# Moving SyncE's second load ahead of its opening-barrier instruction in a decode kernel

## The chip, the cores and the metric

The kernel runs on one core of a Trainium2 chip. The metric is the device time of one execution in microseconds (us). Most executions of one kernel agree within about 0.3%, but some fall into a slower state that is about 8 us longer. A run is called slow when it is over 1.5% above the fastest of the same kernel.

## The reference, cut to what matters

One decode step of a conditioned transformer block, for a batch of 8: a modulation from `c`, attention of one new token over a cache of 8192 positions (32 query heads, 4 key/value heads), and a gated MLP, all bf16.

```python
mod = (silu(c) @ w_mod).reshape(8, 6, 1, -1)          # w_mod: 1024 x 6144, 12 MB
sa, ca, ga, sb, cb, gb = (mod[:, i] for i in range(6))
h = layernorm(x) * (1 + ca) + sa
x = x + ga * attention(h, k_cache, v_cache, wq, wo)   # caches: 2 x 64 MB
h = layernorm(x) * (1 + cb) + sb
x = x + gb * mlp(h, W_gate, W_up, W_down)             # 3 x 7 MB
```

Every weight and cache byte is read once: 185.6 MB. (In the comments of the code an MB is 2^20 bytes; in the text MB and GB are decimal.) That is nearly all of the work.

## The kernel before

All large loads go through SyncE, in one fixed order, into one buffer in SBUF (the on-chip memory) called `arena`. The first three load `w_mod`. The first of them is small.

```python
load(("wm", 0),  wm_src[:, 0:D], D, 0)              # load 1: 128 rows of 2 KB,  256 KB
load(("wm0", 0), wm_src[:, D:24 * D], 23 * D, D)    # load 2: 128 rows of 46 KB, 5888 KB
load(("wm", 1),  wm_src[:, 24 * D:48 * D], 24 * D, 24 * D)   # load 3: rows of 48 KB, 6144 KB
# then wq in two halves; the second half overwrites part of w_mod's first half, so it
# waits until the first w_mod matmuls are done; then K and V of each batch, wo, gate, up, down
```

ScalarE issues two loads of 16 KB for `c` and `x`, 32 rows of 512 B each. The matmuls on `w_mod` need a vector that is computed from `c`; on the tensor engine they also stand behind the layernorm of `x`.

A program opens with a barrier. Each engine gives a signal (its drain instruction), GpSimd collects the signals and releases all, and each engine waits for the release (an EventSemaphore). A helper moves the first loads, which need no wait, ahead of this barrier:

```python
def start_loads_first(nc, n):
    ...
    for engine, ahead, total in ((SP, 1, n), (Activation, 2, 2)):   # names shortened
        ...
        first = [...][:total]                       # the first `total` loads of this engine
        ...
        at = where(rest, engine, "EventSemaphore")[0]
        rest = rest[:at] + first[ahead:] + rest[at:]            # ahead of the barrier's wait
        at = where(rest, engine)[0]
        block.instructions = rest[:at] + first[:ahead] + rest[at:]   # ahead of the drain too
...
start_loads_first(nc, 3)
```

So before the change SyncE runs: load 1, drain, load 2, load 3, wait.

Of the kernel before, what the change touches and what calls it, by code (L numbers as in the profile page):

```python
# [236 lines left out]
def start_loads_first(nc, n):  # L237

    block = nc.main_func.blocks[0]

    def where(ins, engine, opcode=None):
        return [i for i, x in enumerate(ins) if x.engine == engine and opcode in (None, x.opcode)]

    for engine, ahead, total in ((mybir.EngineType.SP, 1, n), (mybir.EngineType.Activation, 2, 2)):
        ins = list(block.instructions)
        at = where(ins, engine, "EventSemaphore")[0]
        first = [ins[i] for i in where(ins, engine) if i > at][:total]
        assert all(x.opcode == "DMACopy" and not x.sync_info.on_wait for x in first), [x.opcode for x in first]
        names = {x.name for x in first}
        rest = [x for x in ins if x.name not in names]  # L250
        at = where(rest, engine, "EventSemaphore")[0]
        rest = rest[:at] + first[ahead:] + rest[at:]
        at = where(rest, engine)[0]
        block.instructions = rest[:at] + first[:ahead] + rest[at:]
# [9 lines left out]
def bass_adaLN_cond__gqa_block_cached__glu_gated_reglu__decode_kernel(nc, A_x, A_k_cache, A_v_cache, A_wq, A_wo, B_x, B_W_gate, B_W_up, B_W_down, c, w_mod, out):  # L264
# [28 lines left out]
    with ExitStack() as es:  # L293
# [483 lines left out]
        P.plan()  # L777
        P.emit(nc, dict(sp=nc.sync, act=nc.scalar, pool=nc.gpsimd, dve=nc.vector, pe=nc.tensor), sems)
        start_loads_first(nc, 3)
        hold_weights(nc, holding)  # L780

# [27 lines left out]
```

## Time and profile before

| what | value |
|---|---|
| time, median of the first 3 runs | 436.74 us (436.25 to 444.89; the last is a slow run) |
| span of the profiled run | 435.1 us |
| bytes moved by DMA, mean rate | 185.74 MB, 427 GB/s |
| slices of 40 in which the DMA engines are at least 90% busy | 38 |

The page of the kernel before. The digits of the DMA row are the busy share of each fortieth of the span in tenths, and the row below is the rate in GB/s.

```profile
span 435.1 us, 4774 instructions
...
DMA  9999999999999999999999999999999999899995
GB/s 374 425 458 434 429 434 434 477 387 473 401 428 434 476 398 428 434 476 392 434 440 470 392 434 440 431 431 476 398 428 434 476 398 470 386 429 481 393 416 232
...
q1 hardware_dynamic: 5360, 185.61, 98.9%
```

SyncE's queue (q1) alone fills the 16 DMA engines for 98.9% of the span. The first slice moves 374 GB/s, less than its neighbours: that is the start-up, and the change is aimed at it.

The timeline of the kernel before, in pieces: start in us, duration in us, engine, source line, operation and count. SPq and ACTq are instructions that SyncE and ScalarE issue.

```profile
0.00 0.39 SPq L391 DMA_DIRECT2D arena<-in_w_mod_dram  x1
0.12 0.40 ACTq L423 DMA_DIRECT2D cx<-in_c_dram  x1
0.56 0.44 ACTq L423 DMA_DIRECT2D cx<-in_A_x_dram  x1
0.64 0.33 SPq L391 DMA_DIRECT2D arena<-in_w_mod_dram  x1
1.02 0.42 SPq L391 DMA_DIRECT2D arena<-in_w_mod_dram  x1
...
1.42 0.20 POOL L433 MEMSET identf<- 128x128 f32 x1 [0.98 <-POOLq L794]
...
8.58 0.58 PE L447 MATMUL ps<-cx,rsel 32*128 32x512 bf16 x1 [8.58 <-DMA cx<-in_A_x_dram]
...
23.38 0.33 SPq L391 DMA_DIRECT2D arena<-in_A_wq_dram  x1
```

Load 2 issues at 0.64. The first work after the barrier (GpSimd's memset) starts at 1.42. The first matmul waits for `x` until 8.58. The second half of `wq` can be issued only at 23.38, after the first `w_mod` matmuls.

The drains of the opening barrier in the same kernel (count, duration in ns, start in us to a tenth):

```profile
L794 SPq DRAIN  x1: 126/126/126, 0.4 to 0.4; - x1
L794 ACTq DRAIN  x1: 150/150/150, 1.0 to 1.0; - x1
```

The loads of the opening: size in KB, and us from issue to landing.

```profile
arena<-in_w_mod_dram SPq DMA_DIRECT2D x1, 5888.0 KB, 16.5
...
arena<-in_w_mod_dram SPq DMA_DIRECT2D x1, 256.0 KB, 2.7
...
cx<-in_A_x_dram ACTq DMA_DIRECT2D x1, 16.0 KB, 7.9
```

The 16 KB load of `x` takes 7.9 us to land because its packets take turns with 46 KB rows: on each engine its two rows and its closing packet of 4 B start at 4.1 to 4.6, 5.9 to 6.3 and 7.6 to 8.1 us, one after each row of load 2.

The trace also holds a record of each DMA packet (start, duration, size, queue). One row is one packet here. A 47,104-byte row at full speed takes 1.74 us on its engine. The records do not name the engine. Each load ends on each engine with a 4-byte packet, so the 16 ends of load 1 and the 16 first rows of load 2 can be sorted and set side by side:

```
kernel before, ns from the first issue, sorted:
load 1, its 4-byte packet ends:  1892 1953 2007 2053 2078 2092 2136 2146 2196 2207 2220 2267 2273 2334 2385 2391
load 2, its first row starts:    1942 2003 2057 2103 2127 2142 2186 2196 2246 2257 2270 2317 2323 2434 2469 2487
```

In 13 of the 16 pairs the row starts 49 or 50 ns after the packet that ends load 1, and in the other three 84 to 100 ns after it. (Sorted pairs need not be of one engine.) The 50 ns are not idle. The records show the load of `c` in them: two packets of 512 B and one of 4 B on each engine.

### The profile page before, as it was taken

To read this page: it belongs to the slowest core of one execution; us is meant where nothing else is said; L and a number is where in the kernel's file an instruction comes from. 1 tells how busy PE (TensorE), PEld (TensorE's weight loads), DVE (VectorE), ACT (ScalarE), POOL (GpSimd) and SP (SyncE) were. 2 spreads that over 40 slices of the span, in tenths; PEclk is the share of its full clock that TensorE was granted. 3 is DMA by queue.
4 is the path that set the end of the run, shared out by engine and by line. 5 is a ranking of instruction groups with operands and counts; after the bars stand their busy time and mean duration, and the time that the engine had idled before them with its cause. 6 is when DMAs were issued, how large, how long until landed. Compare 5 with 4: busy or idle time off the path is not lost. (4 is left out here: it accounts for less than half of the span.)

```text
span 435.1 us, 4774 instructions
## 1 busy us (share of the span) xinstructions
PE 259.8 (60%) x2139; PEld 136.1 (31%) x1979; DVE 249.3 (57%) x342; ACT 29.5 (7%) x54; POOL 8.8 (2%) x22
## 2 busy tenths in 40 slices
PE   0425239667837875883887478487837857263056
PEld 0100003164217224521822352183236217140015
DVE  1503049757972985697299549739963974421020
ACT  2000010100020001002000200200020020100000
POOL 3000000000000000000000000000000000000000
PEclk9976658969978995998799699869979997775669
DMA  9999999999999999999999999999999999899995
GB/s 374 425 458 434 429 434 434 477 387 473 401 428 434 476 398 428 434 476 392 434 440 470 392 434 440 431 431 476 398 428 434 476 398 470 386 429 481 393 416 232
DMA packets 5494, 185.74 MB, mean 427 GB/s; under 512 B 656, under 2 KB 752, under 8 KB 1136
## 3 DMA queue, kind: packets, MB, share of 16 engines
q1 hardware_dynamic: 5360, 185.61, 98.9%
q8 instruction: 5, 0.08, 0.1%
q10 hardware_dynamic: 128, 0.04, 0.0%
q14 instruction: 1, 0.01, 0.0%
HBM read 185.63 MB, written 0.02 MB: 427 GB/s over the span
## 5 line engine op out<-in xcount | busy, mean ns | idle before, releaser
L576 DVE STREAM_TRANSPOSE kt<-arena 128x1024 uint32<-128x1024 uint32 x128 | 148.5, 1213 | 61.2 <-DVEq L181 44.6
L586 PE MATMUL ps<-kt,qpad 128*128 128x512 bf16 x512 | 134.2, 385 | 43.0 <-DVE kt L576 37.2
L626 PE MATMUL ps<-arena,pT 128*64 128x256 bf16 x1024 | 72.5, 315 | 51.4 <-PEq L181 51.4
L626 PEld LDWEIGHTS ps<-arena,pT 128*64 128x64 bf16 x1024 | 70.1, 129 | 53.2 <-issue 52.7
L586 PEld LDWEIGHTS ps<-kt,qpad 128*128 128x128 bf16 x512 | 40.8, 99 | 132.5 <-DVE kt L576 98.9
L616 DVE TENSOR_SCALAR pT<-pd,mqf 128x1024 bf16<-128x1024 bf16 x64 | 28.2, 503 | 0.6
L608 ACT ACTIVATE prb<-ps,bias 128x1024 bf16<-128x1024 f32 x16 | 17.7, 1110 | 138.3 <-DVE mjt L603 138.3
L614 DVE STREAM_TRANSPOSE pd<-prb 128x1024 bf16<-128x1024 bf16 x16 | 19.8, 1239 | 10.9 <-ACT prb L608 10.9
L592 DVE TENSOR_REDUCE negm<-ps 128x1 f32<-128x512 f32 x32 | 21.2, 662 | 4.5 <-PE ps L586 4.5
L744 PE MATMUL ps<-arena,hT 128*32 128x448 bf16 x128 | 10.6, 514 | 18.4 <-DMA arena<-in_B_W_up_dram 11.6
L751 DVE TENSOR_TENSOR kt<-ps,kt 128x448 bf16<-128x448 f32 x2 | 1.2, 619 | 27.9 <-PE ps L744 27.9
L514 PE MATMUL ps<-arena,hT 128*32 128x512 bf16 x96 | 10.6, 631 | 8.3 <-DMA arena<-in_w_mod_dram 8.3
L538 PE MATMUL ps<-arena,hT 128*32 128x512 bf16 x64 | 6.8, 604 | 12.3 <-DMA arena<-in_A_wq_dram 12.3
L645 ACT ACTIVATE oacc<-ps 128x32 f32 (+1 forms) x9 | 1.8, 198 | 157.7 <-PE ps L640 157.7
L521 DVE COPY mod<-ps 128x512 f32<-128x512 f32 x2 | 1.3, 670 | 18.3 <-PE ps L514 18.3
L567 POOL TENSOR_TENSOR qpad<-qR,mq 128x128 bf16<-128x128 bf16 x8 | 4.9, 609 | 311.0 <-DVE pT L616 257.8
L744 PEld LDWEIGHTS ps<-arena,hT 128*32 128x32 bf16 x64 | 2.3, 137 | 26.5 <-DMA arena<-in_B_W_up_dram 12.3
L763 PE MATMUL ps<-arena,hmT 128*32 128x256 bf16 x112 | 8.1, 306 | 3.9 <-DMA arena<-in_B_W_down_dram 3.9
L549 DVE CAST kt<-ps 128x512 bf16<-128x512 f32 x1 | 0.7, 692 | 15.6 <-PE ps L538 15.6
L714 PE MATMUL ps<-arena,kt 128*32 128x256 bf16 x128 | 5.7, 362 | 5.1 <-DMA arena<-in_A_wo_dram 5.1
L598 PE MATMUL ps<-identf,negm 128*128 128x128 f32 x16 | 3.9, 326 | 7.8 <-DVE negm L596 7.8
L763 PEld LDWEIGHTS ps<-arena,hmT 128*32 128x32 bf16 x112 | 6.5, 109 | 5.9 <-DMA arena<-in_B_W_down_dram 5.3
(87 smaller groups left out, 79.7 us busy)
## 6 DMA issues: line engine op xcount, KB each, us to landing
arena<-in_A_k_cache_dram SPq DMA_DIRECT2D x16, 4096.0 KB, 27.1
arena<-in_A_wq_dram SPq DMA_DIRECT2D x2, 4096.0 KB, 34.4
arena<-in_B_W_gate_dram SPq DMA_DIRECT2D x1, 7168.0 KB, 25.0
arena<-in_B_W_up_dram SPq DMA_DIRECT2D x1, 7168.0 KB, 28.1
arena<-in_w_mod_dram SPq DMA_DIRECT2D x1, 6144.0 KB, 30.6
arena<-in_w_mod_dram SPq DMA_DIRECT2D x1, 5888.0 KB, 16.5
arena<-in_B_W_down_dram SPq DMA_DIRECT2D x1, 3584.0 KB, 20.0
arena<-in_B_W_down_dram SPq DMA_DIRECT2D x1, 1792.0 KB, 23.9
```

The source lines that it names most:

```text
L514: fns.append(lambda e, w=w, pr=pr, j=j, kk=kk: hold(e.matmul(ps[32 * j:32 * j + 32, pr, :], hT[:, kk, :], w[:, 2 * pr:2 * pr + 2, j, :], s ...
L538: fns.append(lambda e, w=w, r=kk - r0, z=z, g=g, kk=kk: hold(e.matmul(ps[32 * g:32 * g + 32, 4 + z, :], hT[:, kk, :], w[:, r, g, z, :], st ...
L576: P.op("dve", lambda e_: e_.transpose(ktb[:, to:to + PART].bitcast(dt.uint32), arena[:, lo:lo + PART].bitcast(dt.uint32)), reads=[slot_r(l ...
L586: fns.append(lambda e_, t=t, r=r: e_.matmul(ps[:, e // 4, :].rearrange("p (c k) -> p c k", k=32), qpad[:, t * 2 + r, 24 - 8 * i:152 - 8 * ...
L592: P.op("dve", lambda e: e.tensor_reduce(negm[:, h:h + 1], ps[:, h, :], AX.X, ALU.max, negate=True), reads=[bank(h)] + (free(("ka", b)) if ...
L608: P.op("act", lambda e: e.activation(prb[:, f, :], ps[:, 2 * f:2 * f + 2, :].rearrange("p h n -> p (h n)"), ACT.Exp, bias=bias[:, 0:1], sc ...
L614: P.op("dve", lambda e: e.transpose(pd[:, f], prb[:, f]), reads=[R("prb", f, f + 1)], writes=[R("pd", 1024 * f, 1024 * f + 1024)])
L616: P.op("dve", lambda e, g=g: e.tensor_scalar(out=pT[:, f, :, :, g, :], in0=pd[:, f].rearrange("p (c i x) -> p c i x", c=32, i=2), scalar1= ...
L626: fns.append(lambda e, n=n, h=h, c_=c_, i=i, t=t: e.matmul(ps[64 * t:64 * t + 64, 5, 0:2 * Dh].rearrange("p (i d) -> p i d", d=Dh), pT[:, ...
L714: fns.append(lambda e, w=w, k=k, j=j: e.matmul(ps[32 * j:32 * j + 32, 5, 0:256], oX[:, k, :], w[:, k, j, :], start=(k == 0), stop=(k == KO ...
L744: fns.append(lambda e, w=w, kk=kk, h=h, j=j, b0=b0: hold(e.matmul(ps[32 * j:32 * j + 32, b0 + h, 0:H], hT[:, kk, :], w[:, kk, j, h, :], st ...
L763: fns.append(lambda e, w=w, r=k - r0, k=k, i2=i2, j=j: e.matmul(ps[32 * j:32 * j + 32, 4, 0:256], hmT[:, k, 1 - i2:33 - i2], w[:, r, i2, j ...
```

## The change

The intent is to let SyncE issue its first big load before it spends time on the barrier.

```diff
-    for engine, ahead, total in ((mybir.EngineType.SP, 1, n), (mybir.EngineType.Activation, 2, 2)):
+    for engine, ahead, total in ((mybir.EngineType.SP, 2, n), (mybir.EngineType.Activation, 2, 2)):
```

SyncE now runs: load 1, load 2, drain, load 3, wait. No instruction is added or removed.

## The prediction

> **What bounds the kernel now.** DMA. The page gives 185.74 MB at a mean of 427 GB/s and a DMA share of 9 tenths or more in 38 of 40 slices. In the packet records a 47,104-byte row takes 1.74 us on one of 16 engines (together 433 GB/s), and in the first 10 us each engine's next row starts as its last one ends. So a moved issue is worth only what it moves the start of this stream, or a later stall of it.
>
> **The opening, from the instruction timeline and the packet records (us from the first issue).** SyncE: load 1 (256 KB, 2 KB rows) issues 0.00 to 0.39; its barrier drain 0.44 to 0.57; load 2 (5.9 MB) 0.64 to 0.97; load 3 (6.1 MB) 1.02 to 1.44; its barrier wait 1.50. ScalarE: the loads of c and x 0.13 to 0.53 and 0.56 to 1.00, its drain 1.04 to 1.19. [...] First packet of load 1: 1.02, 0.63 after its issue ended. The Trainium skill, "DMA: Bandwidth & Descriptors", Latency and other measured facts, gives about 600 ns to the first byte on this path; this trace agrees. Load 1's packets end engine by engine at 1.9 to 2.4; load 2's first rows start on the same engines at 1.94 to 2.49.
>
> **What the change does.** It adds and removes nothing. Load 2's issue goes ahead of the drain (0.20 us with the gaps): it starts near 0.43 and ends near 0.77; SyncE's drain moves to 0.82-0.95; load 3 stays near 1.0-1.4.
>
> **What of it is critical.** Almost nothing.
> 1. Load 2 could already begin at about 0.97 + 0.63 = 1.6, before any engine was through load 1 (1.9). After, it could at 1.4, but the engines are as busy with load 1: I expect its start 0 to 0.2 us earlier.
> 2. The barrier is set by ScalarE's drain, ending 1.19; SyncE's then ends at 0.95. Release stays near 1.3; 0.2 us later would cost nothing either.
> 3. x may land a row or two later, because load 2's rows are queued sooner than its 512-byte packets. The same page, Queues, rings and completion order, has the engines alternate between queues packet by packet; the trace agrees (x's packets at 4.1 and 5.9 between 1.74 us rows; x lands at 8.5). c (2.9) could fall behind rows too. That is hidden: the chain from x to the first w_mod matmuls (18.04 to 23.35) gates the second wq half's load, issued 23.38, while the queue holds data until 41.3: slack about 18 us.
>
> So the time is the same minus 0 to 0.2 us.
>
> **Prediction.** 436.5 us, 8 in 10 between 435.4 and 437.7 (runs of one kernel scatter more than the effect). Faster by over 2%: 0.01; within 2%: 0.97; slower by over 2%: 0.02.
>
> **What would show each step.** Timeline: SyncE's second issue near 0.43, before the drain; GpSimd's first memset after the barrier still near 1.4. Packet records: load 2's first rows still start at about 1.9 to 2.5, and load 2 lands (17.2 before) within 0.3 us of that. x's issue to landing: 7.9 before, 7 to 11.5 after; the matmul that reads it (8.58) moves with it, and the second wq half's issue by no more than that. DMA share per slice otherwise as before.
>
> **What would make it wrong.** If the small loads fell behind so many rows (over 15 us) that the stream stalled; if SyncE's drain waited for its DMA work and the barrier came late; if the sequencers' issues contend so that load 1 itself starts later; or if the runs fall in a slow state (one of three was 444.89).

## The result and the profile after

The changed kernel took 436.51 us (median of 6 runs, 436.36 to 444.49), the kernel before 436.85 us (median of 6, 436.25 to 444.89). The ratio of the fast runs is 0.9994, with a 95% interval from 0.9981 to 1.0008: no difference. A ratio here is the mean time of one kernel's fast runs over that of the other's fast runs of the same rounds, so it is not quite the ratio of the medians.

The first profile of the changed kernel fell in the slow state (span 443.1 us), and its DMA rows are not comparable with those of before. The same kernel was therefore run again (first experiment below) and gave a profile in the fast state. That one is shown here. The page:

```profile
span 434.9 us, 4774 instructions
...
DMA  9999999999999999999999999999999999999995
GB/s 374 434 449 434 432 434 437 471 390 473 404 425 434 473 404 425 434 473 395 434 437 470 392 431 443 428 431 473 404 425 434 473 404 464 393 429 454 418 413 239
...
q1 hardware_dynamic: 5360, 185.61, 98.9%
```

The first slice moves 374 GB/s as before, and the queue's share is 98.9% as before. The timeline:

```profile
0.00 0.39 SPq L391 DMA_DIRECT2D arena<-in_w_mod_dram  x1
...
0.44 0.42 SPq L391 DMA_DIRECT2D arena<-in_w_mod_dram  x1
...
1.11 0.33 SPq L391 DMA_DIRECT2D arena<-in_w_mod_dram  x1
1.42 0.20 POOL L433 MEMSET identf<- 128x128 f32 x1 [0.98 <-POOLq L794]
...
8.48 0.58 PE L447 MATMUL ps<-cx,rsel 32*128 32x512 bf16 x1 [8.48 <-DMA cx<-in_A_x_dram]
...
23.28 0.33 SPq L391 DMA_DIRECT2D arena<-in_A_wq_dram  x1
```

Load 2 issues 0.20 us sooner, at 0.44. In these lines nothing else moves by more than 0.1 us. The drains and the loads:

```profile
L794 SPq DRAIN  x1: 125/125/125, 0.9 to 0.9; - x1
L794 ACTq DRAIN  x1: 150/150/150, 1.0 to 1.0; - x1
```

```profile
arena<-in_w_mod_dram SPq DMA_DIRECT2D x1, 5888.0 KB, 16.6
...
cx<-in_A_x_dram ACTq DMA_DIRECT2D x1, 16.0 KB, 7.8
```

SyncE's drain is 0.47 us later but still ahead of ScalarE's, so the barrier releases at the same time. Load 2 is issued 0.20 us sooner and takes 0.1 us longer to land. The packet records show why it gains so little:

```
changed kernel, fast state, ns from the first issue, sorted:
load 1, its 4-byte packet ends:  1915 1938 1960 2017 2071 2085 2087 2122 2126 2217 2277 2309 2339 2346 2352 2391
load 2, its first row starts:    1981 1988 2010 2067 2131 2135 2137 2171 2176 2267 2327 2358 2389 2396 2402 2441
```

Again each row follows load 1 by 49 to 66 ns. Fourteen rows again start about 3 ns before a closing packet of `c` ends, and the other two 7 and 14 ns after one. So the work that the DMA engines still had, and not the issue, sets when load 2 begins, before the change on all but two engines. Before and after, the first rows start at 1.94 to 2.49 and 1.98 to 2.44 us.

### The profile page after: what moved, and what is told of

Its sections match the earlier page's. It is cut to its first block, busy times and chain, and to the rows that moved or that the text cites. A ratio compares the mean times of both kernels' runs of the same rounds, so it can differ in the third digit from the quotient of the medians.

```text
span 443.1 us, 4774 instructions
## 1 busy us (share of the span) xinstructions
PE 263.3 (59%) x2139; PEld 138.0 (31%) x1979; DVE 249.0 (56%) x342; ACT 29.5 (7%) x54; POOL 8.7 (2%) x22
## 3 DMA queue, kind: packets, MB, share of 16 engines
q1 hardware_dynamic: 5360, 185.61, 98.9%
## 5 line engine op out<-in xcount | busy, mean ns | idle before, releaser
L626 PE MATMUL ps<-arena,pT 128*64 128x256 bf16 x1024 | 74.5, 320 | 51.8 <-PEq L181 51.8
L626 PEld LDWEIGHTS ps<-arena,pT 128*64 128x64 bf16 x1024 | 72.0, 132 | 53.7 <-issue 53.1
```

What stands on the lines that cost most here:

```text
L626: fns.append(lambda e, n=n, h=h, c_=c_, i=i, t=t: e.matmul(ps[64 * t:64 * t + 64, 5, 0:2 * Dh].rearrange("p (i d) -> p i d", d=Dh), pT[:, ...
```

## The experiments

Theory A: an engine begins load 2 when it is through with load 1, provided that load 2 is ready by then; it was ready in time before, so an earlier issue only makes it wait longer. Rival B: the issue counts, but the gain is given back by a later `x` or a later barrier. Rival C: the issue counts in proportion and the gain is only too small to see. Theory A allows a one-sided effect: sooner gains nothing, later must cost at some point.

Each run had its own runs of the kernel before on the same chip. Their medians were 436.56, 436.55, 436.52 and 436.48 us in the four groups (runs 1 to 4, 5 to 8, 9 to 11, and 12).

### 1. The changed kernel again

No edit. Expected:

> The changed kernel once more, for a profile in the fast state (its first one fell in the slow state). Theory A (the engines are still busy with load 1 when load 2's rows become ready, so its issue is not what they wait for): load 2 issues near 0.44 us, its first rows still start at 1.9 to 2.5 us, it lands within 0.3 us of 17.2, time within 0.1% of the kernel before. Rival B (the issue does gate load 2, but the gain of 0.2 us is given back through x landing later): first rows start about 0.2 us sooner, near 1.75 to 2.3 us, load 2 lands near 17.0, and a later wait grows. Rival C (the gain is real and only under the noise): rows 0.2 us sooner, no wait grows, the last load lands 0.2 us sooner.

Measured: 436.28 us, ratio 0.9997 (0.9984 to 1.0010). First rows at 1.98 to 2.44 us as A expects. Load 2 landed at 17.06 us, against 17.16. The profiled span is 0.2 us shorter, but a single pair of profiles cannot tell 0.2 us from scatter, so a tiny gain (C) is not excluded; one above 0.16% is, by the interval.

The slow profile of the changed kernel differs in one point:

```profile
10.03 0.58 PE L447 MATMUL ps<-cx,rsel 32*128 32x512 bf16 x1 [10.03 <-DMA cx<-in_A_x_dram]
```

There `x` landed 1.45 us later than before (9.94 against 8.49 us), because on one engine a packet of `x` stood behind one row more. Whether the new order or the slow state did that is open.

### 2. Loads 2 and 3 behind the barrier's wait

```diff
-((mybir.EngineType.SP, 2, n), ...)      start_loads_first(nc, 3)
+((mybir.EngineType.SP, 1, n), ...)      start_loads_first(nc, 1)
```

> Only load 1 goes ahead of the barrier; loads 2 and 3 wait behind it. Load 2 then issues near 1.35 to 1.75 us, ready near 2.4, later than most engines are done with load 1 (1.9 to 2.4). Theory A: now the engines do wait, first rows start near 2.4 to 2.6 instead of 1.9 to 2.5, a loss of 0.1 to 0.4 us, at most 0.1% of the time. Rival B or C (each us of issue counts): a loss of 0.7 us against the kernel before (0.16%).

Measured: 437.80 us, ratio 1.0033 (1.0020 to 1.0046), that is 1.2 us longer than the kernel before. A had expected 0.4 us at most. B and C had expected 0.7 us. The timeline of this kernel:

```profile
1.42 0.33 SPq L391 DMA_DIRECT2D arena<-in_w_mod_dram  x1
...
3.24 0.58 PE L447 MATMUL ps<-cx,rsel 32*128 32x512 bf16 x1 [3.24 <-DMA cx<-in_A_x_dram]
```

```
ns from the first issue, sorted:
load 1, its 4-byte packet ends:  1883 1923 1987 2048 2101 2118 2158 2174 2177 2192 2235 2268 2297 2305 2327 2429
load 2, its first row starts:    2392 2394 2499 2514 2541 2549 2573 2591 2598 2608 2801 2968 3020 3133 3251 3501
```

Now 0.4 to 1.1 us lie between the loads in the sorted pairs. Packets of `c` and `x` fill about 0.1 us of it on each engine, the rest is idle: none of the 16 rows starts directly behind another packet. Two things had been left out of the expectation. The rows do not become ready at one time: the last engine's row starts 2.1 us after the issue began, the first 1.0 us. And a first row that starts on idle engines is slower: the 16 first rows took 2.41 us on average, against 2.08 before and 1.95 in the changed kernel. Note also that `x` was read 5.3 us sooner here (3.24 against 8.58), because no large rows were in its way, and the kernel was slower all the same. So rival B has the priorities wrong: an earlier `x` did not make up for the later stream.

### 3. No load ahead of the barrier

```diff
-for engine, ahead, total in ((mybir.EngineType.SP, 2, n), (mybir.EngineType.Activation, 2, 2)):
+for engine, ahead, total in ((mybir.EngineType.Activation, 2, 2),):
```

> No SyncE load ahead of the barrier. Theory A and the bound by DMA: the first packet moves from 1.02 to about 2.2 us after ScalarE's first issue, and the time grows by 1.0 to 1.4 us (0.25 to 0.3%), since nothing later in the stream can win it back. If the stream has slack instead, the time stays within 0.1%.

Measured: 437.86 us, ratio 1.0031 (1.0018 to 1.0044), as expected. Load 1 is issued at 1.43 us and the first packet comes at 2.45. The first rows of load 2 start at 3.38 to 3.82 us, again right behind load 1: `c` had landed by then, and 15 of the 16 rows start about 3 ns before a closing packet of load 1 ends.

### 4. Four loads ahead of the drain

```diff
-((mybir.EngineType.SP, 2, n), ...)      start_loads_first(nc, 3)
+((mybir.EngineType.SP, 4, n), ...)      start_loads_first(nc, 4)
```

> Four SyncE loads ahead of both its drain and its wait. SyncE's drain then ends near 1.9 us and becomes the last of the barrier, so the other engines leave near 2.1 instead of 1.35 us. Theory (the barrier is off the critical path): GpSimd's first memset after it near 2.1 instead of 1.42 us, the time within 0.1%. Rival (barrier counts): 0.7 us longer, 0.16%.

Measured: 436.41 us, ratio 0.9998 (0.9984 to 1.0011). The drains and the timeline of this kernel:

```profile
L794 ACTq DRAIN  x1: 150/150/150, 1.0 to 1.0; - x1
L794 SPq DRAIN  x1: 125/125/125, 1.9 to 1.9; - x1
```

```profile
2.21 0.20 POOL L433 MEMSET identf<- 128x128 f32 x1 [1.77 <-POOLq L794]
...
8.54 0.58 PE L447 MATMUL ps<-cx,rsel 32*128 32x512 bf16 x1 [8.54 <-DMA cx<-in_A_x_dram]
```

SyncE's drain is now the last, the barrier releases 0.8 us later (2.21 against 1.42), and neither the first matmul nor the time moves. The barrier is off the critical path. One thing does not fit theory A fully: although load 2 was issued at 0.44 us, on one engine its first row came only at 2.86 us, 0.53 us after the packet before it. Run 10 has one such engine too (3.33 us, in a slow profile). Why is not shown; the cost of one late engine is too small to see in the times.

### 5. `c` and `x` held back behind six memsets

```diff
+for _ in range(6):      # scr: an unused 128 x 1024 bf16 tile; ScalarE's two loads now read it
+    P.op("pool", lambda e: e.memset(scr[:], 0.0), reads=[R("scr")], writes=[R("scr")])
```

> The loads of c and x are held back behind six extra GpSimd memsets (about 11 us). Claim of the prediction: slack of about 18 us behind x. So the matmul that reads x starts near 18 to 21 us instead of 8.6, the first w_mod matmuls near 28 to 31, the second wq half's load is issued near 34 to 36 while the queue holds data until about 41, and the time is the same within 0.2%. Rival (x's arrival counts, so that a later x gives a gain back): about 10 us longer, 2.3%.

The cut leaves out that the two loads also move from the opening to behind the memsets, so that ScalarE issues nothing ahead of the barrier (the same in runs 6 and 10).

Measured: 438.07 us, ratio 1.0017 (1.0001 to 1.0032), but with five times of 443.00, 437.32, 438.07, 436.58 and 438.93 us. The second half of `wq` was issued at 38.95 us, later than expected, because `x` now took 13.1 us to land between large rows. The 443.00 belongs to the profiled run, and that profile has the mark of the slow state (394 GB/s between 20 and 100 us, where a fast run of the changed kernel has 432; see the last section), although its time is just under the limit for that label. With the queue dry at about 41 us this run had used up nearly all of its slack, so the result was inconclusive.

### 6. The same with 24 memsets

```diff
-for _ in range(6):
+for _ in range(24):
```

> The same with 24 memsets (about 29 us). The second wq half's load is then issued near 50 to 55 us, about 9 to 13 us after the queue ran dry at 41. Claim: the time grows by that overrun, 8 to 14 us (2 to 3%), not by the whole 28 us; the DMA share shows a hole at about 41 to 52 us. Rival (slack is larger than read): same time.

Measured: 453.20 us, ratio 1.038 (1.0364 to 1.0396): 16.65 us longer, more than the 8 to 14 expected. The page and the timeline of this kernel:

```profile
DMA  9995099998998998999999999999999999999996
GB/s 411 424 418 234 0 416 418 461 459 380 442 473 383 449 467 389 449 461 394 444 423 432 458 409 438 452 409 441 449 412 441 447 452 441 406 448 426 428 405 248
```

```profile
41.34 0.58 PE L450 MATMUL ps<-cx,rsel 32*128 32x512 bf16 x1 [41.34 <-DMA cx<-in_A_x_dram]
...
55.94 0.33 SPq L392 DMA_DIRECT2D arena<-in_A_wq_dram  x1
```

The DMA row drops to 5 and 0 in the fourth and fifth slices (34 to 57 us): the hole. The issue of the second `wq` half came 32.66 us later than in run 1 (55.94 against 23.28), and 16.65 us of that showed in the time. The slack was thus 16.0 us. The prediction had read about 18 us. The mechanism held; the size was off. The prediction counted up to 41.3 us, when the last queued load lands. In the records of this run the engines run dry at 40.6 to 41.2 us (mean 40.9), and their next rows start at 56.9 to 57.5 us (mean 57.1), 1.0 to 1.6 us after the issue. So an engine is idle for 16.2 us on average. That leaves 0.5 us; the first rows after the hole are slower (1.78 us on average for 32 KB, later 1.21), which would fit, but no run separates it.

### 7. The whole stream held back

```diff
+for _ in range(6):      # ahead of all other work of GpSimd; every SyncE load now reads scr
+    P.op("pool", lambda e: e.memset(scr[:], 0.0), reads=[R("scr")], writes=[R("scr")])
```

> All SyncE loads wait for six GpSimd memsets, so the first is issued about 7 us into the program. Claim (the stream's start counts one for one): the time grows by what the first packet is later, 6 to 8 us (1.4 to 1.8%). Rival (part is won back later): under 4 us.

The cut leaves out that no SyncE load goes ahead of the barrier here.

Measured: 443.73 us, ratio 1.0164 (1.0148 to 1.0179). Load 1 was issued at 7.44 us and the time grew by 7.18 us (443.73 minus 436.55). The start of the stream counts one for one, as expected.

### 8. Loads 1 and 2 as one load

```diff
-load(("wm", 0), wm_src[:, 0:D], D, 0)
-load(("wm0", 0), wm_src[:, D:24 * D], 23 * D, D)
+load(("wm", 0), wm_src[:, 0:24 * D], 24 * D, 0)     # issued first, ahead of the drain
```

> Loads 1 and 2 become one of 48 KB rows, issued ahead of the drain. Theory A says that load 2's rows waited for the engines, not for their issue or for their size: first rows start near 1.0 us, right where load 1's packets started, and the first w_mod half lands sooner than 17.2 by what load 1's small packets cost beyond their bytes, up to 0.5 us. Time 0 to 0.5 us shorter, not resolvable at 0.1%. Rival (big rows can't start sooner than about 1.9 us whatever lies ahead): first rows near 1.9 us, time 0.3 us longer. c and x land later, each of their packets behind rows of 1.8 us, without effect.

Measured: 436.65 us, ratio 1.0001 (0.9988 to 1.0015). Half of the expectation held. The big rows started at 1.01 to 1.84 us, so size alone does not keep them from starting. But the first half of `w_mod` did not land sooner: its last row ended at 17.23 us, against 16.79 before, and on average an engine was through with it at 16.60 us, against 16.53. The first rows took 2.45 us on average instead of 1.82, so the start-up loss is there with one large load as well. The small load 1 of the kernel before does not speed up the stream, but it lets `x` land early (first matmul at 8.58, here at 14.06).

### 9. Only load 3 behind the wait

```diff
-((mybir.EngineType.SP, 2, n), ...)      start_loads_first(nc, 3)
+((mybir.EngineType.SP, 1, n), ...)      start_loads_first(nc, 2)
```

> Separates load 2 from load 3 in the run that put both behind the barrier and lost 1.2 us. Load 2 stays where it was before the change (between SyncE's drain and wait, near 0.64 us); only load 3 goes behind the wait (near 1.4 us). Theory A: load 3 is not needed before about 16 us, so load 2's first rows are at 1.9 to 2.5 us as before and the time is within 0.1%. Rival (load 3 cost it, or the mere issuing after the wait): 1 us longer, 0.25%.

Measured: fast runs 436.68, 436.26, 436.45, 440.94 and 437.40 us, ratio 1.0029 with a wide interval (0.9986 to 1.0071) that the 440.94 makes. The interval settles nothing. The packet records say more: load 2's first rows start at 1.96 to 2.38 us, as before, 15 of the 16 directly behind a closing packet of `c`, and three of the five times are at or below 436.7. So the late first rows of run 2 do not come from load 3's place. That load 3 costs no time at all is likely, but the scatter of this run leaves it unproven.

### 10. `c` and `x` behind one memset

```diff
-for _ in range(6):
+for _ in range(1):
```

> The loads of c and x wait behind one extra GpSimd memset instead of six: issued near 6.4 us. The run with six left only about 2 us between the second wq half's issue (38.95) and the queue running dry (41 to 43), and its five times scattered from 436.6 to 443.0. If that scatter came from the used-up slack, here the second wq half is issued near 33 to 36 us, and the times lie within 0.3 us of the kernel before, with its usual scatter. If x's arrival counts in itself, 0.2% or more is lost here too.

Measured: 436.50 us, ratio 1.0001 (0.9987 to 1.0015); the fast runs lie between 436.19 and 437.02. The first matmul started at 19.97 us and the second `wq` half was issued at 34.44 us (in a slow profile). So a delay of 11 us in reading `x` costs nothing that can be seen. The scatter of run 5 went away with the slack restored, which fits but does not prove that it came from there, as the unprofiled runs of run 5 have no trace.

### 11. Load 2 at about 1 us

```diff
 # c's load goes from ScalarE to SyncE, between loads 1 and 2
-P.op("act", lambda e, t=t, src=src: e.dma_start(cx[:, t, :], src), ...)
+P.op(("sp", "act")[t], lambda e, t=t, src=src: e.dma_start(cx[:, t, :], src), ...)
```

> A dose between: c's load moves from ScalarE to SyncE, between loads 1 and 2, so load 2 issues near 1.05 us instead of 0.64 (before) or 1.42 (the run that lost 1.2 us). Ready near 2.0 us, when the first engines are done with load 1 but the slowest (2.4) are not. Theory A (per engine, a row starts at the later of load 1's end plus 0.05 us and load 2's readiness): first rows 2.05 to 2.5 us, the slowest unmoved, time within 0.1%. Rival (each us of later issue costs in proportion, 1.2 us per 0.78 us): 0.6 us longer, 0.15%.

The cut leaves out the changes to the helper. SyncE runs: load 1, drain, `c`, load 2, load 3, wait; ScalarE: `x`, drain, wait.

```profile
1.03 0.41 SPq L391 DMA_DIRECT2D arena<-in_w_mod_dram  x1
```

Measured: 437.56 us, ratio 1.0026 (1.0013 to 1.0039): 1.0 us longer. A had expected no loss and C 0.6 us; both missed. Load 2 issued at 1.03 us, and its first rows started at 2.30 to 3.36 us and took 2.36 us on average, much as in run 2. One row of the 16 starts directly behind another packet, against 14 before. So 0.38 us later than before is already too late.

### 12. The losing order with a larger load 1

```diff
 # on top of run 2
-load(("wm", 0), wm_src[:, 0:D], D, 0)
-load(("wm0", 0), wm_src[:, D:24 * D], 23 * D, D)
+load(("wm", 0), wm_src[:, 0:4 * D], 4 * D, 0)              # rows of 8 KB
+load(("wm0", 0), wm_src[:, 4 * D:24 * D], 20 * D, 4 * D)   # rows of 40 KB
```

> The losing order (loads 2 and 3 behind the barrier wait, load 2 issued near 1.42 us) with a larger load 1: 8 KB rows instead of 2 KB, so load 1 keeps the engines busy until about 3.9 to 4.4 us; load 2 has 40 KB rows. Theory A (an engine loses only if load 2 is not ready when it is through with load 1; in the losing runs the last engine's row started 2.1 to 2.3 us after the issue, here 3.5 to 3.7): load 2's first rows start 0.05 to 0.1 us after load 1's end on each engine, and the loss of 1.2 us is gone, time within 0.1% of the kernel before. Rival (an issue behind the barrier costs its 0.8 to 1.2 us whatever covers it): 0.25 to 0.3% longer, as without the larger load 1.

Measured: 437.01 us, ratio 1.0013 (0.9998 to 1.0027), between the two expectations: 0.5 us of loss instead of 1.2. Load 1 now ends at 4.11 to 4.53 us, and load 2's first rows start 0.05 to 0.16 us behind it on 14 engines but 0.36 and 0.57 us behind on the last two (in sorted pairs). Part of the 0.16 us is again filled by packets of `c` and `x`: 11 rows start directly behind one. More cover takes away most of the idle time and more than half of the loss. That supports A, and it speaks against C: the issue is as late as in run 2, and the loss is not the same. The rest is open: the last two rows come 3.5 and 3.7 us after the issue, later than the 2.1 us of run 2 would lead one to expect.

### All runs on one scale

The last end of a row of `w_mod`'s first half is when the slowest engine is through with the opening. It comes from one profile of each kernel, and the times are medians.

| kernel | load 2 issued, us | its first rows start, us | last row of w_mod's first half ends, us | time, us |
|---|---|---|---|---|
| changed (run 1) | 0.44 | 1.98 to 2.44 | 16.75 | 436.28 |
| before | 0.64 | 1.94 to 2.49 | 16.79 | 436.48 to 436.56 |
| four loads ahead (4) | 0.44 | 1.93 to 2.86 | 16.81 | 436.41 |
| load 3 behind (9) | 0.64 | 1.96 to 2.38 | 17.07 | 436.68 |
| one big load (8) | 0.00 | 1.01 to 1.84 | 17.23 | 436.65 |
| larger load 1 (12) | 1.42 | 4.16 to 5.09 | 17.58 | 437.01 |
| load 2 at 1 us (11) | 1.03 | 2.30 to 3.36 | 18.03 | 437.56 |
| loads 2 and 3 behind (2) | 1.42 | 2.39 to 3.50 | 18.12 | 437.80 |
| none ahead (3) | 1.87 | 3.38 to 3.82 | 18.50 | 437.86 |
| stream late (7) | 7.88 | 9.25 to 9.82 | 24.20 | 443.73 |

The time follows the fourth column almost one for one: from the first to the last line 7.45 us there and 7.45 us in time. Most of that is run 7; without it the two are 1.75 and 1.58 us. The mean end over the 16 engines gives the same order but for run 4. The time does not follow the second column. No version was clearly faster than the two kernels; the changed one and the one before are level.

## Why the prediction was right

The prediction was 436.5 us with "the same" at 0.97, and the time was 436.51. That the two agree to 0.01 us is luck: the fast runs of the changed kernel lie between 436.36 and 436.94. The mechanism was right, with two sizes off. Point by point:

- "What bounds the kernel now. DMA." Shown. A stream that starts 7.44 us later costs 7.18 us (run 7), and a hole in it costs about its length (16.65 us for 16.2, run 6).
- "The engines are as busy with load 1": shown in the records, though these do not name the engines. Before and after the change 14 of the 16 first rows start as another load's closing packet ends. The two latest rows before were up to 0.1 us late.
- "Load 2 could already begin at about 0.97 + 0.63 = 1.6." This step was too generous. It took the 0.63 us that load 1's first packet showed for a delay that holds for all 16 engines. Where the engines were idle (runs 2 and 11), the first row came 1.0 to 1.3 us after the issue began and the last 2.1 to 2.3 us after it. Nor is this a fixed delay: with load 1 still running, single engines took 2.4 us (run 4) to 3.7 us (run 12). The kernel before had less than 0.38 us to spare, since an issue 0.38 us later lost 1.0 us (run 11, which also moved c's load), and on its two latest engines it had nothing to spare. The error did no harm because the change moves the issue to the safe side.
- "The barrier is set by ScalarE's drain": shown. Release at 1.42 in both, and a release 0.8 us later costs nothing (run 4).
- "x may land a row or two later": in the fast profile it did not; 7.8 us to landing against 7.9. In the slow one it landed a row later on one engine. That it would not matter was right (run 10).
- "Slack about 18 us": measured 16.0 us (run 6). The sum took the landing of the last load for the time when the queue is dry (0.4 us too late on average) and left out the 1.1 us from the issue to the next rows.
- The expected gain of 0 to 0.2 us: the fast runs allow anything from a gain of 0.16% to a loss of 0.10% (run 1), so its size stays open. On average an engine was through with the first half of `w_mod` at 16.42 us in runs 1 and 4, against 16.53 before, which would fit a gain of 0.1 us but does not show it.

Two statements of the Trainium skill's page "DMA: Bandwidth & Descriptors" bear on this. Its section Issuing engines are not separate DMA queues says that starting DMAs on several engines at once saves only the sequencer's time for the issue, which is usually small beside the DMA itself. The change here moves an issue on one engine, so only the comparison of sizes carries over, and it agrees: an issue of 0.33 to 0.42 us stands beside about 14 us of rows (8 of 1.74 us on each engine). Run 11 shows its limit: an issue that comes 0.38 us too late costs 1.0 us. The section Queues, rings and completion order has each engine take turns between queues packet by packet. This trace agrees, with one row as a packet: between the rows of load 2 each engine sends one packet of `x` at a time. So `x` lands after 2.6 us with no large rows queued (run 2), 7.9 us behind 46 KB rows, and 13.1 us in run 5.

## What to carry to other kernels

When the DMA engines are the bottleneck, ask of each issue whether the engines will be idle when it becomes ready, and read that from the packets of the load ahead of it, not from the issue instructions. Moving an issue that is already covered gains nothing, while the same issue 0.4 us later cost 1 us here, so the margin is worth measuring in the direction in which it hurts. A load's readiness should be counted for its slowest engine.

## What the Trainium skill lacked or had wrong

- "DMA: Bandwidth & Descriptors", Latency and other measured facts: it gives about 600 ns to the first byte on this path, and load 1's first packet came 0.63 us after its issue ended. The page does not say from where to count (1.02 us from the issue's start), nor over what stretch the 16 engines begin; another page, "Perfetto Trace Analysis", draws the engines' beginnings apart (DMA Instruction — HWDGE) but gives no times. Here, with the engines done with load 1, the first rows of one load started at 2.39 to 3.50 us, for an issue at 1.42 (run 2). What an engine does in between is not in the trace.
- The same page (DMA) has no start-up slowness of the rows themselves. The first 47,104-byte row of each engine took 1.95 to 2.41 us on average (runs 1 and 2), later ones 1.74 us; the first 49,152-byte rows 2.45 us (run 8), later ones 1.82.
- The same page, Where 436 GB/s comes from, says that for HBM to SBUF the HBM side (about 358 GB/s) binds. Taken alone this is wrong for this case: here the stream held 433 GB/s over 300 us. The page's own table (425 GB/s for 16 MB), which it gives for a single core with the other core of its pair idle, is the better guide.
- No page that was read tells of the slow state of a single core. In the changed kernel, in a fast run (run 1) and in its first profile (slow), it looks as follows. The columns after the stretch are the busy time of each engine, the granted TensorE clock, the DMA share and GB/s:

```profile
20.00:100.00 80.00, 43.16 (x342) 17.57 (x254) 33.49 (x47) 4.97 (x8) 1.08 (x2) 0.72 1.00 432
100.00:400.00 300.00, 196.49 (x1562) 108.73 (x1552) 204.80 (x271) 20.37 (x40) 3.79 (x6) 0.88 1.00 433
```

```profile
20.00:100.00 80.00, 35.76 (x237) 9.29 (x139) 33.39 (x48) 4.97 (x8) 1.08 (x2) 0.73 0.99 392
100.00:400.00 300.00, 205.00 (x1660) 118.54 (x1656) 203.68 (x270) 19.75 (x39) 3.78 (x6) 0.87 1.01 435
```

The slow run loses its time mainly between 20 and 100 us, where the DMA rate is 392 instead of 432 GB/s (80 us x (432 - 392) / 392 = 8 us, and it is 8.2 us longer). After that the rates are alike, and the granted clock is the same within 0.01. The slow profile of run 10 has 386 GB/s in the same stretch. So in these two profiles the slow state is one of the DMA rate in the first 100 us, not of the TensorE clock; the cause is not known.
